# Program order in the first stage of a gated attention and MLP kernel: high halves of splits ahead of low halves, layernorm transposes moved, last stores on three queues

## The chip, the cores and the metric

The kernel runs on one core of a Trainium2 chip. The core has TensorE (PE, matmuls; its weight loads are listed apart as PEld), VectorE (DVE), ScalarE (ACT), GpSimd (POOL) and SyncE (SP, which here only issues DMAs). Each engine takes its instructions in the order of the program. The metric is the device time of one execution in microseconds (us).

## What is computed

With x of 2048 x 448 (all float32), 16 heads of 28, one shared key and value head, and g a sigmoid of x times a gate vector:

```python
q = (x @ wq).reshape(B, S, H, Dh).transpose(0, 2, 1, 3)
k = x @ wk
v = x @ wv
p = softmax(einsum("bhqd,bkd->bhqk", q, k) * Dh ** -0.5)
a = einsum("bhqk,bkd->bhqd", p, v).transpose(0, 2, 1, 3).reshape(B, S, H * Dh) @ wo

h = gelu(layernorm(x) @ w1)
hs = shifted(h) @ w2          # the four quarters of h moved by +1, -1, +2, -2 rows
x1 = x + hs
b = x1 + gelu(layernorm(x1) @ w3) @ w4

out = g * a + (1 - g) * b
```

## The kernel before

The kernel has three stages: q, k, v and the spatial mixer (stage one, to about 140 us), the channel MLP (to about 400 us), and attention with the output projection. The change touches stage one and the last few instructions of stage three.

**Splits.** A float32 product is made of three matmuls of rounded operands: high x high, high x low, low x high. So each operand is split: ACT casts it to its high half (wh, ah, w2h), and DVE subtracts that from the raw value for the low half (wl, al, w2l). `split_w` does it for w1 (high casts, then four subtractions), `split_a` and `split_x` for chunks c0 to c1 of a block of x, `split_w2(m)` for chunk m of w2.

**Blocks.** x is worked in four blocks of 512 rows, b = 0 to 3. `load_x(b)` brings the transposed block (xkv_b), `load_x1(b)` the plain one (x1). The high half of a block stands in a tile `ah` and its low half in `al`, three buffers each, so block 3 takes over those of block 0.

**Steps.** In program order:

- `stage_q(u)`, u = 4b + g: 11 matmuls (`proj`) for 128 columns of q, k and v of block b; `q_out` copies the result on ACT to one of four buffers qf and stores it on ACT's queue to DRAM (qd).
- `ln1_tile(b, t)`: layernorm statistics of tile t of block b on DVE; after t = 3 POOL computes the four scales rs (`stats_end`). The mean is taken out of w1 beforehand (`centre_w1`), so that only rs remains.
- `ln1_send(b)`: PE transposes rs (rsT_b), ACT copies it (rT_b), SP stores it to DRAM. `ln1_read(b)`: SP reads it back as rsb_b, broadcast to 112 partitions.
- `stage_w1(b, between)`: four tiles h_b_m (m = 0 to 3), 11 matmuls each; after each of them `between(m)` is called, then DVE multiplies the result by rsb_b (hf_b_m), ACT takes the Gelu twice (hh, the high half, and hf), and POOL subtracts (hl).
- `stage_w2(b, between)`: four tiles hs_b_t, 12 matmuls each on hh and hl of all four m; DVE adds each to x1, then `between(t)` is called. Tile 3 also reads the first columns of the next block, which POOL copies (L396).
- `stage_kv(b)`: SP reads k and v of block b back from DRAM; `split_k(b)` splits k on POOL.

PE's PSUM tiles for q and h go round four buffers. Everything is in manual schedule: each engine's order is the order of the code, and an instruction waits for what its operands and buffers need.

**The code from q6 to hs_0** calls, before the change: `stage_q(6)`, `centre_w1`, `stage_q(7)`, `split_w` of w1, four `ln1_tile(1, t)`, `stage_q(8)`, `ln1_send(0)`, `stage_q(9)`, `ln1_send(1)`, both `ln1_read`, the loads of block 3, `stage_q(10)`, `stage_q(11)`, `stage_w1(0, split_w2)`, `stage_w1(1, second)`, `stage_kv(0)`, `stage_kv(1)`, `stage_w2(0, third)`. `second(m)` splits block 3 for m = 0 and 1 and takes statistics of block 2 for m = 2 and 3; `third(0)` sends and reads the scales of block 2 and reads k and v of it, `third(1)` to `third(3)` take statistics of block 3.

**The end.** The last four tiles of the output (12 to 15) are computed one after the other; DVE writes 12, 14 and 15, ACT and POOL together 13. Tile 12 is stored from SP's queue, the other three from POOL's. After that every engine loads the flag `redo` (L935) and branches on it (L938) past a repeat of the attention that is not taken in the runs here.

Of the kernel before, what the change touches and what calls it, by code (L numbers as in the profile page):

```python
# [10 lines left out]
F32R = mybir.dt.float32r  # L11
# [5 lines left out]
P = 128  # L17
# [19 lines left out]
def f32(ap):  # L37
    return ap.bitcast(F32)
# [3 lines left out]
def gated_mix_kernel(  # L42
# [12 lines left out]
    nc = tc.nc  # L55
# [20 lines left out]
    first = keep.tile([P, 4], F32, name="first")  # L76
# [28 lines left out]
            nc.vector.tensor_tensor(wl[0:64, 3, cols], raw[0:64, 3, cols], f32(wh)[0:64, 3, cols], ALU.subtract)  # L105
            nc.scalar.copy(wl[64:128, 3, cols], raw[64:128, 3, cols])

    def split_w(raw, wh, wl):
        nc.scalar.copy(wh[:, 0:3, :], raw[:, 0:3, :])
        nc.gpsimd.memset(f32(wh)[64:128, 3, :], 0.0)  # L110
        nc.scalar.copy(wh[0:64, 3, :], raw[0:64, 3, :])
        nc.scalar.copy(wl[64:128, 3, :], raw[64:128, 3, :])
        for c in range(3):
            nc.vector.tensor_tensor(wl[:, c, :], raw[:, c, :], f32(wh)[:, c, :], ALU.subtract)
        nc.vector.tensor_tensor(wl[0:64, 3, :], raw[0:64, 3, :], f32(wh)[0:64, 3, :], ALU.subtract)

    def split_a(raw, ah, al, c0, c1):
        nc.scalar.copy(ah[:, c0:c1, :], raw[:, c0:c1, :])
        c2 = min(c1, 3)
        if c0 < c2:  # L120
            nc.vector.tensor_sub(al[:, c0:c2, :], raw[:, c0:c2, :], f32(ah)[:, c0:c2, :])
        if c1 == 4:
            nc.vector.tensor_sub(ah[64:128, 3, :], raw[64:128, 3, :], f32(ah)[64:128, 3, :])
# [110 lines left out]
    with tc.tile_pool(name="s1b", bufs=1) as s1b, \  # L234
# [13 lines left out]
        xraw, xact = {}, {}  # L248

        def load_x(b):  # L250
            xraw[b] = s1.tile([P, 4, 512], F32, tag="raw", bufs=3, name=f"xkv_{b}")
            nc.sync.dma_start(xraw[b], xT[:, :, 512 * b:512 * b + 512])

        def load_x1(b):
            nc.sync.dma_start(x1[:, 4 * b:4 * b + 4, :],
                              x[512 * b:512 * b + 512, :].rearrange("(t p) d -> p t d", p=P))
# [12 lines left out]
        w2l = s1b.tile([P, 4, D], F32R, name="w2l")  # L269
        hh, hl, acts = {}, {}, {}  # L270

        def split_x(b, c0, c1):
            if b not in xact:
                xact[b] = (s1.tile([P, 4, 512], F32R, tag="ah", bufs=3, name=f"ahk_{b}"),
                           s1.tile([P, 3, 512], F32R, tag="al", bufs=3, name=f"alk_{b}"))
            split_a(xraw[b], *xact[b], c0, c1)

        def q_out(u, ps):
            b, g = divmod(u, NG)
# [16 lines left out]
        def stage_q(u, tile_of=mm1):  # L296
            b, g = divmod(u, NG)
            ps = tile_of(f"q_{u}")
            w = slice(g * P, (g + 1) * P)
            proj(ps, wqh[:, :, w], wql[:, :, w], *xact[b])  # L300
            q_out(u, ps)
# [34 lines left out]
        def ln1_tile(b, t):  # L336
            if t == 0:
                rs1_of[b] = stats_tiles(s1, b)
            stats_tile(s1, b, t, rs1_of[b][0])
            if t == 3:  # L340
                stats_end(*rs1_of[b])

        def ln1_send(b):
            ps = misc_tile(f"rsT_{b}")[0:4, 0:P]
            nc.tensor.transpose(ps, rs1_of.pop(b)[1], ident)
            rT = s1.tile([4, P], F32, tag="rT", bufs=2, name=f"rT_{b}")
            nc.scalar.copy(rT, ps)
            rb_of[b] = dram.tile([4, P], F32, tag="rsd", bufs=2, name=f"rsd_{b}")
            nc.sync.dma_start(rb_of[b], rT)

        def ln1_read(b):
            rd = rb_of[b]
            rb_of[b] = s1.tile([P, 512], F32, tag="rsb", bufs=2, name=f"rsb_{b}")
            nc.sync.dma_start(rb_of[b][0:C], rd.rearrange("(o t) p -> o (t p)", o=1).broadcast_to([C, 512]))
# [14 lines left out]
                nc.vector.scalar_tensor_tensor(w1raw[:, c, :], ps, -1.0 / D, w1raw[:, c, :],  # L369
                                               op0=ALU.mult, op1=ALU.add)  # L370

        def split_w2(m):
            nc.scalar.copy(w2h[0:C, m, :], w2raw[0:C, m, :])
            nc.vector.tensor_tensor(w2l[0:C, m, :], w2raw[0:C, m, :], f32(w2h)[0:C, m, :], ALU.subtract)

        def stage_w1(b, between=None):
            hh[b] = s1b.tile([P, 4, 516], F32R, tag="hh", bufs=2, name=f"hh_{b}")
            hl[b] = s1b.tile([P, 4, 516], F32R, tag="hl", bufs=2, name=f"hl_{b}")
            for m in range(4):
                ps = mm1(f"h_{b}_{m}")  # L380
                w = slice(m * C, (m + 1) * C)
                proj(ps[0:C, :], w1h[:, :, w], w1l[:, :, w], *xact[b])
                if between:
                    between(m)
                hf = s1.tile([P, 512], F32, tag="hf", bufs=3, name=f"hf_{b}_{m}")
                nc.vector.tensor_mul(hf[0:C, :], ps[0:C, :], rb_of[b][0:C, :])
                nc.scalar.activation(hh[b][0:C, m, 2:514], hf[0:C, :], AF.Gelu_apprx_tanh)
                nc.scalar.activation(hf[0:C, :], hf[0:C, :], AF.Gelu_apprx_tanh)
                nc.gpsimd.tensor_tensor(hl[b][0:C, m, 2:514], hf[0:C, :], f32(hh[b])[0:C, m, 2:514],
                                        ALU.subtract)  # L390
            for tt in (hh, hl):
                if b == 0:
                    nc.gpsimd.memset(f32(tt[b])[0:C, :, 0:2], 0.0)
                else:
                    nc.gpsimd.tensor_copy(tt[b][0:C, :, 0:2], f32(tt[b - 1])[0:C, :, 512:514])
                    nc.gpsimd.tensor_copy(tt[b - 1][0:C, :, 514:516], f32(tt[b])[0:C, :, 2:4])  # L396
                if b == NB - 1:
                    nc.gpsimd.memset(f32(tt[b])[0:C, :, 514:516], 0.0)
# [43 lines left out]
        stage_q(6)  # L442
        centre_w1()
        stage_q(7)
        split_w(w1raw, w1h, w1l)
        for t in range(4):
            ln1_tile(1, t)
        stage_q(8)
        ln1_send(0)
        stage_q(9)  # L450
        ln1_send(1)
        ln1_read(0)
        ln1_read(1)
        load_x(3)
        load_x1(3)
        stage_q(10)
        stage_q(11)
        stage_w1(0, split_w2)

        def second(m):  # L460
            if m < 2:
                split_x(3, 2 * m, 2 * m + 2)
            else:
                ln1_tile(2, 2 * m - 4)
                ln1_tile(2, 2 * m - 3)
# [3 lines left out]
        stage_kv(1)  # L469

        def third(t):
            if t == 0:
                ln1_send(2)
                ln1_read(2)
                stage_kv(2)
            else:
                ln1_tile(3, t - 1)

        stage_w2(0, third)
        ln1_tile(3, 3)  # L480
        split_k(0)
        mv0, rs0 = stats_tiles(s1, "m")
# [186 lines left out]
    with tc.tile_pool(name="s3", bufs=1, reuse_waits="tile") as s3, \  # L669
# [220 lines left out]
        def end(t, n, ps, before):  # L890
            if t == 1:
                nc.scalar.activation(y, ps, AF.Copy, scale=gg[:, n:n + 1])
                nc.gpsimd.tensor_tensor(ot_of[n], y, before, ALU.add)
            else:
                nc.vector.scalar_tensor_tensor(ot_of[n], ps, gg[:, n:n + 1], before, op0=ALU.mult, op1=ALU.add)
            queue = nc.sync if t == 0 else nc.gpsimd
            queue.dma_start(out[0, n * P:(n + 1) * P, :], ot_of[n])

        def tail_wo(t):
# [112 lines left out]
```

## Time and profile before

| | us |
|---|---|
| runs of the kernel, median of 3 | 977.44 |
| lowest and highest | 976.42 and 979.18 |
| the profiled execution's own time | 977.92 |
| its span, from the first instruction to the last | 976.1 |
| PE busy | 954.6 (98%) |
| ACT busy | 648.5 (66%) |
| DVE busy | 288.0 (30%) |
| POOL busy | 114.1 (12%) |

Busy times are sums over the span, and stages differ: from 400 to 940 us PE is busy throughout and ACT for 495 of 540 us; from 30 to 60 us PE is busy for 24.84 of 30 us, and from 60 to 80 us for 14.00 of 20. A row of the timeline gives the start, the duration, the engine, the line, the operation and its tiles (out<-in), and in brackets the idle time of the engine before it with what ended it. Matmuls are pipelined: their durations overlap, and the distance of two starts is what one of them costs PE. SPq and ACTq are queues of DMA issues.

### The profile page before, as it was taken

The page shows a single profiled execution, that of the slowest core. Times are in us where ns is not written, and L with a number is a line of the kernel's source. Part 1 is how long each engine was busy: PE and PEld are TensorE (multiplying, and loading weights), DVE is VectorE, ACT ScalarE, POOL GpSimd, SP SyncE. Part 2 cuts the span into 40 slices and gives each one's busy share as a digit, 9 for nine tenths or more (in the row PEclk, how much of TensorE's full clock was granted, in tenths as well). Part 3 has the DMA queues.
Part 4 walks back from the last instruction along what each step waited for, and adds up shares of the span by engine and source line. Part 5 has one row for each costly group of instructions (what it writes and reads, how often), then busy time and mean ns, then how long its engine had stood idle before and what let it go on. Part 6 is the DMA issues. An engine that isn't in the chain of part 4 may idle for free.

```text
span 976.1 us, 13516 instructions
## 1 busy us (share of the span) xinstructions
PE 954.6 (98%) x5191; PEld 636.0 (65%) x5191; DVE 288.0 (30%) x573; ACT 648.5 (66%) x1266; POOL 114.1 (12%) x139
## 2 busy tenths in 40 slices
PE   9779999999999999999999999999999999999996
PEld 6658888888888888855555555555555555545553
DVE  5454354642431431122122222212222221212102
ACT  5352235432232232289999999999999999999994
POOL 3133230200000520040000000000000000000001
PEclk9898999999999999999999999999999999999999
DMA  9810533131120110020110121011021101210101
GB/s 310 260 37 21 137 129 122 41 92 29 26 56 2 38 43 1 10 76 22 40 51 16 36 87 41 22 39 51 22 68 50 42 21 40 69 46 17 40 12 42
DMA packets 44200, 56.24 MB, mean 58 GB/s; under 512 B 9536, under 2 KB 27280, under 8 KB 44128
## 3 DMA queue, kind: packets, MB, share of 16 engines
q1 hardware_dynamic: 41056, 49.37, 17.6%
q10 hardware_dynamic: 2880, 5.24, 1.5%
q8 instruction: 43, 0.70, 0.3%
q0 software_dynamic: 192, 0.69, 0.2%
q14 instruction: 29, 0.24, 0.1%
HBM read 32.19 MB, written 11.67 MB: 45 GB/s over the span
## 4 chain that ended last, share of the span: by engine, by line
PE 93%; ACT 2%; DVE 2%; DMA 1%; issue 1%; POOL 1%; ACTq 0%; POOLq 0%; DVEq 0%
PE bank L831 27%; PE pv L800 24%; PE acc L608 5%; PE acc L610 5%; PE acc L609 5%; PE g L127 4%; PE g L128 4%; PE g L129 4%; PE hs L405 1%; PE hs L406 1%; PE hs L407 1%; PE bank L746 1%; PE bank L744 1%; PE g L130 1%; PE bank L742 1%; PE g L131 1%
## 5 line engine op out<-in xcount | busy, mean ns | idle before, releaser
L833 ACT ACTIVATE p<-bank 128x512 f32<-128x512 f32 x1024 | 511.5, 639 | 34.1 <-PE bank L831 30.9
L831 PE MATMUL bank<-qs,kS 98*128 98x512 f32 x1024 | 306.0, 408 | 0.0
L831 PEld LDWEIGHTS bank<-qs,kS 98*128 98x128 f32 x1024 | 184.3, 189 | 134.1 <-issue 93.1
L800 PE MATMUL pv<-p,vext 128*32 128x512 f32 x2048 | 243.1, 598 | 0.0
L598 ACT ACTIVATE gh<-g 128x512 fp32r<-128x512 f32 x55 | 32.9, 598 | 183.1 <-PE g L131 183.1
L800 PEld LDWEIGHTS pv<-p,vext 128*32 128x32 f32 x2048 | 58.5, 109 | 116.3 <-issue 108.6
L600 DVE TENSOR_TENSOR gl<-gf,gh 128x512 fp32r<-128x512 f32 x55 | 38.3, 696 | 162.5 <-ACT gf L599 158.3
L608 PE MATMUL acc<-w4h,gh 128*128 128x448 f32 x220 | 79.9, 363 | 0.0
L610 PE MATMUL acc<-w4h,gl 128*128 128x448 f32 x220 | 79.9, 363 | 0.0
L609 PE MATMUL acc<-w4l,gh 128*128 128x448 f32 x220 | 79.7, 362 | 0.0
L754 DVE SCALAR_TENSOR_TENSOR ot<-bank,gg,ot 128x448 f32<-128x448 f32 x44 | 30.0, 684 | 143.0 <-ACT p L833 99.3
L127 PE MATMUL g<-ah,w3h 128*128 128x512 f32 x168 | 65.7, 391 | 0.0
L128 PE MATMUL g<-al,w3h 128*128 128x512 f32 x168 | 65.6, 391 | 0.0
L129 PE MATMUL g<-ah,w3l 128*128 128x512 f32 x168 | 65.6, 391 | 0.0
L729 POOL CAST onh<-on 128x512 fp32r<-128x512 f32 x15 | 9.2, 611 | 472.8 <-DVE on L726 472.8
L204 DVE TENSOR_REDUCE mr<-bank 128x4 f32<-128x256 f32 x60 | 25.6, 426 | 105.8 <-PE bank L203 104.7
L609 PEld LDWEIGHTS acc<-w4l,gh 128*128 128x128 f32 x220 | 41.3, 188 | 4.2
L608 PEld LDWEIGHTS acc<-w4h,gh 128*128 128x128 f32 x220 | 41.3, 188 | 4.1
L610 PEld LDWEIGHTS acc<-w4h,gl 128*128 128x128 f32 x220 | 41.3, 188 | 3.0
L708 DVE COPY o<-pv 128x512 f32<-128x512 f32 x15 | 10.4, 692 | 99.4 <-PE pv L800 99.4
L129 PEld LDWEIGHTS g<-ah,w3l 128*128 128x128 f32 x168 | 31.5, 188 | 6.9
L128 PEld LDWEIGHTS g<-al,w3h 128*128 128x128 f32 x168 | 31.5, 188 | 5.6
(193 smaller groups left out, 981.2 us busy)
## 6 DMA issues: line engine op xcount, KB each, us to landing
qs<-qh SPq DMA_DIRECT2D x32, 224.0 KB
qd<-qf ACTq DMA_DIRECT2D x16, 256.0 KB
rb<-rd SPq DMA_DIRECT2D x15, 256.0 KB
x<-in_x_dram SPq DMA_DIRECT2D x4, 896.0 KB
xd<-xt SPq DMA_DIRECT2D x16, 224.0 KB
w34raw<-in_w_dram SPq DMA_DIRECT2D x7, 512.0 KB
qr<-qd SPq DMA_DIRECT2D x16, 224.0 KB
qs<-ql SPq DMA_DIRECT2D x16, 224.0 KB
```

What stands on the lines that cost most here:

```text
L127: nc.tensor.matmul(ps, wh[:, c, :], ah[:, c, :], start=(c == 0), stop=False)
L128: nc.tensor.matmul(ps, wh[:, c, :], al[:, c, :], start=False, stop=False)
L129: nc.tensor.matmul(ps, wl[:, c, :], ah[:, c, :], start=False, stop=False)
L598: nc.scalar.activation(gh, ps, AF.Gelu_apprx_tanh)
L600: nc.vector.tensor_sub(gl, gf, f32(gh))
L608: nc.tensor.matmul(ps, gh[:, tok], w4h[i][:, k, :], start=(f == 0), stop=False)
L609: nc.tensor.matmul(ps, gh[:, tok], w4l[i][:, k, :], start=False, stop=False)
L610: nc.tensor.matmul(ps, gl[:, tok], w4h[i][:, k, :], start=False, stop=(f == stop))
L754: nc.vector.scalar_tensor_tensor(ot_of[n], ps, gg[:, n:n + 1], before, op0=ALU.mult, op1=ALU.add)
L800: nc.tensor.matmul(pv[32 * j:32 * j + 32, :], vext[:, kt, :], ps[j], start=(kt == 0), stop=(kt == NT - 1), tile_position=(0, 32 * j))
L831: nc.tensor.matmul(ps, kS[0:98, kt * P:(kt + 1) * P], q_of[u][0:98, j, :], start=True, stop=True)
L833: nc.scalar.activation(p, ps, AF.Exp, scale=SCALE)
```

## The change

Four things are done.

1. `split_w`, `split_a` and `split_w2` are cut into a high part (ACT) and a low part (DVE), so that they can stand apart in the program. w2's casts for m = 0 and 1 go ahead of `stage_w1(0)`, those for m = 2 and 3 are called after h_0_0 and h_0_1, and block 3's casts (`high_x`) after h_0_2 and h_0_3, where they were in `stage_w1(1)`.
2. `stage_q(8)`, `ln1_send(0)` and `ln1_read(0)` go ahead of w1's split; w1's casts go ahead of the statistics of block 1, w1's subtractions behind them.
3. The transpose of block 1's scales goes from behind q9 to behind h_0_2, with its read; that of block 2's scales from behind hs_0_0 to behind hs_0_2. `stage_kv(2)` goes behind `stage_w2(0)`, and the statistics of block 3 a tile earlier.
4. Of the last four stores, tile 13's stays on POOL's queue, tiles 14 and 15 go to ACT's.

```diff
-    def split_w(raw, wh, wl):
+    def split_w_high(raw, wh, wl):
         nc.scalar.copy(wh[:, 0:3, :], raw[:, 0:3, :])
         nc.gpsimd.memset(f32(wh)[64:128, 3, :], 0.0)
         nc.scalar.copy(wh[0:64, 3, :], raw[0:64, 3, :])
         nc.scalar.copy(wl[64:128, 3, :], raw[64:128, 3, :])
+
+    def split_w_low(raw, wh, wl):
         for c in range(3):
             nc.vector.tensor_tensor(wl[:, c, :], raw[:, c, :], f32(wh)[:, c, :], ALU.subtract)
         nc.vector.tensor_tensor(wl[0:64, 3, :], raw[0:64, 3, :], f32(wh)[0:64, 3, :], ALU.subtract)
...
+        def high_x(b, c0, c1):
+            if b not in xact:
+                xact[b] = (s1.tile([P, 4, 512], F32R, tag="ah", bufs=3, name=f"ahk_{b}"),
+                           s1.tile([P, 3, 512], F32R, tag="al", bufs=3, name=f"alk_{b}"))
+            nc.scalar.copy(xact[b][0][:, c0:c1, :], xraw[b][:, c0:c1, :])
...
-        def split_w2(m):
+        def high_w2(m):
             nc.scalar.copy(w2h[0:C, m, :], w2raw[0:C, m, :])
+
+        def low_w2(m):
             nc.vector.tensor_tensor(w2l[0:C, m, :], w2raw[0:C, m, :], f32(w2h)[0:C, m, :], ALU.subtract)
...
         stage_q(6)
         centre_w1()
         stage_q(7)
-        split_w(w1raw, w1h, w1l)
+        stage_q(8)
+        ln1_send(0)
+        ln1_read(0)
+        split_w_high(w1raw, w1h, w1l)
         for t in range(4):
             ln1_tile(1, t)
-        stage_q(8)
-        ln1_send(0)
+        split_w_low(w1raw, w1h, w1l)
         stage_q(9)
-        ln1_send(1)
-        ln1_read(0)
-        ln1_read(1)
         load_x(3)
+        stage_q(10)
         load_x1(3)
-        stage_q(10)
         stage_q(11)
-        stage_w1(0, split_w2)
+        high_w2(0)
+        high_w2(1)
+
+        def first(m):
+            low_w2(m)
+            if m < 2:
+                high_w2(m + 2)
+            else:
+                high_x(3, 2 * m - 4, 2 * m - 2)
+            if m == 2:
+                ln1_send(1)
+                ln1_read(1)
+
+        stage_w1(0, first)
 
         def second(m):
             if m < 2:
-                split_x(3, 2 * m, 2 * m + 2)
+                split_x(3, 2 * m, 2 * m + 2, False)
...
         def third(t):
-            if t == 0:
+            if t == 2:
                 ln1_send(2)
                 ln1_read(2)
-                stage_kv(2)
-            else:
-                ln1_tile(3, t - 1)
+            if t < 3:
+                ln1_tile(3, t)
 
         stage_w2(0, third)
+        stage_kv(2)
         ln1_tile(3, 3)
...
-            queue = nc.sync if t == 0 else nc.gpsimd
+            queue = (nc.sync, nc.gpsimd, nc.scalar, nc.scalar)[t]
             queue.dma_start(out[0, n * P:(n + 1) * P, :], ot_of[n])
```

PE's order before, at the end of q9 (lines of the kernel before; a number behind a name, as in q_9_366, is a running one):

```order
L130 MATMUL q_9_366<-ahk_2_230,wqh_118 128x512
L131 MATMUL q_9_366<-ahk_2_230,wql_119 128x512
L345 MATMUL rsT_1_381<-ident_67,rs_s1_1_330 4x128
L127 MATMUL q_10_394<-ahk_2_230,wqh_118 128x512
L128 MATMUL q_10_394<-alk_2_231,wqh_118 128x512
```

PE's order now, where that transpose has gone, between the third and the fourth tile of h_0 (lines of the kernel after, where 345 is 358, 127 is 134 and 131 is 138):

```order
L137 MATMUL h_0_2_458<-ahk_0_143,w1h_130 112x512
L138 MATMUL h_0_2_458<-ahk_0_143,w1l_131 112x512
L358 MATMUL rsT_1_474<-ident_67,rs_s1_1_349 4x128
L134 MATMUL h_0_3_487<-ahk_0_143,w1h_130 112x512
L135 MATMUL h_0_3_487<-alk_0_144,w1h_130 112x512
```

The transpose rsT_1 has moved behind q10, q11 and three tiles of h_0; h_0_3 behind it still reads ahk_0, the high half of block 0.

DVE's order before, from the centring of w1 (w1l is w1's low half, st and mv the statistics, here of block 1):

```order
L369 SCALAR_TENSOR_TENSOR w1raw_141<-wsum_ps_300,w1raw_141 128x448 x4
L114 TENSOR_TENSOR w1l_131<-w1raw_141,w1h_130 128x448 x3
L115 TENSOR_TENSOR w1l_131<-w1raw_141,w1h_130 64x448
L135 BN_STATS st_s1_1_0_331<-x1_74 128x6
L136 BN_AGGR mv_s1_1_329<-st_s1_1_0_331 128x2
```

And now:

```order
L382 SCALAR_TENSOR_TENSOR w1raw_141<-wsum_ps_300,w1raw_141 128x448 x4
L142 BN_STATS st_s1_1_0_350<-x1_74 128x6
L143 BN_AGGR mv_s1_1_348<-st_s1_1_0_350 128x2
L142 BN_STATS st_s1_1_1_353<-x1_74 128x6
L143 BN_AGGR mv_s1_1_348<-st_s1_1_1_353 128x2
L142 BN_STATS st_s1_1_2_356<-x1_74 128x6
L143 BN_AGGR mv_s1_1_348<-st_s1_1_2_356 128x2
L142 BN_STATS st_s1_1_3_359<-x1_74 128x6
L143 BN_AGGR mv_s1_1_348<-st_s1_1_3_359 128x2
L116 TENSOR_TENSOR w1l_131<-w1raw_141,w1h_130 128x448 x3
L117 TENSOR_TENSOR w1l_131<-w1raw_141,w1h_130 64x448
```

The four pairs of statistics have gone ahead of the four subtractions, which need ACT's casts.

ACT's order before, from the Gelus of h_0_1, with the waits of each row in brackets (the engine or the DMA semaphore; a row without one needs no wait of its own):

```order
L387 ACTIVATE hh_0_424<-hf_0_1_459 112x512 [waits DVE_49]
L388 ACTIVATE hf_0_1_459<-hf_0_1_459 112x512 [waits Activation_49]
L373 CAST w2h_132<-w2raw_205 112x448
L387 ACTIVATE hh_0_424<-hf_0_2_478 112x512 [waits DVE_49]
L388 ACTIVATE hf_0_2_478<-hf_0_2_478 112x512 [waits Activation_49,Pool_49]
L373 CAST w2h_132<-w2raw_205 112x448
L387 ACTIVATE hh_0_424<-hf_0_3_497 112x512 [waits DVE_49]
```

And now, from the same Gelus:

```order
L402 ACTIVATE hh_0_418<-hf_0_1_453 112x512 [waits DVE_49]
L403 ACTIVATE hf_0_1_453<-hf_0_1_453 112x512 [waits Activation_49]
L289 CAST ahk_3_471<-xkv_3_383 128x1024 [waits DMAHW3_49,PE_49]
L360 COPY rT_1_476<-rsT_1_474 4x128
L402 ACTIVATE hh_0_418<-hf_0_2_482 112x512 [waits DVE_49]
L403 ACTIVATE hf_0_2_482<-hf_0_2_482 112x512 [waits Activation_49,Pool_49]
L289 CAST ahk_3_471<-xkv_3_383 128x1024
L402 ACTIVATE hh_0_418<-hf_0_3_501 112x512 [waits DVE_49]
```

Between the Gelus w2's casts have made room for block 3's casts, the first of which waits for PE, and for the copy of rsT_1, which now stands behind that cast.

More of the change, by code (lines that the diff above doesn't have):

```diff
@@ L115, in split_w, with split_a @@
         nc.vector.tensor_tensor(wl[0:64, 3, :], raw[0:64, 3, :], f32(wh)[0:64, 3, :], ALU.subtract)
-    def split_a(raw, ah, al, c0, c1):
-        nc.scalar.copy(ah[:, c0:c1, :], raw[:, c0:c1, :])
+    def split_w(raw, wh, wl):
+        split_w_high(raw, wh, wl)
+        split_w_low(raw, wh, wl)
+    def split_a(raw, ah, al, c0, c1, high=True):
+        if high:
+            nc.scalar.copy(ah[:, c0:c1, :], raw[:, c0:c1, :])
         c2 = min(c1, 3)
@@ L270, in gated_mix_kernel, with split_x @@
         hh, hl, acts = {}, {}, {}
-        def split_x(b, c0, c1):
+        def split_x(b, c0, c1, high=True):
             if b not in xact:
@@ L275, in split_x @@
                            s1.tile([P, 3, 512], F32R, tag="al", bufs=3, name=f"alk_{b}"))
-            split_a(xraw[b], *xact[b], c0, c1)
+            split_a(xraw[b], *xact[b], c0, c1, high)
+        def high_x(b, c0, c1):
[3 more added lines that the diff above has]
+            nc.scalar.copy(xact[b][0][:, c0:c1, :], xraw[b][:, c0:c1, :])
         def q_out(u, ps):
```

## The prediction

> **What bounds the kernel now.** I read the page's line of granted clock first, then the waits of TensorE (PE), then its timeline from 31 to 84 us. The fence shows the clock in 40 slices; one line of the waits of PE from 20 to 100 us (total, times, longest); two stretches with busy time by engine, granted clock and DMA share; and PE matmuls with start, duration and, in brackets, the idle time before.
>
> ```profile
> PEclk9898999999999999999999999999999999999999
> ...
> PE rsT L345 <- POOL rs_s L140: 11.2, 2, 6.0
> ...
> 37.38:41.95 4.57, 4.56 (x12) 3.60 (x13) 0.00 (x0) 0.26 (x1) 0.00 (x0) 0.50 0.43 95
> 73.57:79.50 5.93, 5.92 (x17) 5.33 (x18) 1.03 (x2) 0.26 (x1) 1.54 (x5) 0.50 0.10 39
> ...
> 31.84 0.39 PE L131 MATMUL q<-ahk,wql 128*128 128x512 f32 x1
> 37.39 0.38 PE L345 MATMUL rsT<-ident,rs_s 128*4 128x128 f32 x1 [5.16 <-POOL rs_s L140]
> 42.13 0.40 PE L127 MATMUL q<-ahk,wqh 128*128 128x512 f32 x1
> 44.65 0.39 PE L127 MATMUL h<-ahk,w1h 128*112 128x512 f32 x1
> 64.96 0.37 PE L405 MATMUL hs<-w2h,hh 112*128 112x448 f32 x1
> 73.58 0.37 PE L345 MATMUL rsT<-ident,rs_s 128*4 128x128 f32 x1 [6.00 <-POOL rs_s L140]
> 79.84 0.37 PE L407 MATMUL hs<-w2h,hl 112*128 112x448 f32 x1
> 83.50 0.37 PE L407 MATMUL hs<-w2h,hl 112*128 112x448 f32 x1
> 83.71 0.40 PE L127 MATMUL h<-ahk,w1h 128*112 128x512 f32 x1
> ```
>
> PE is the bound nearly everywhere. It stops twice, 5.16 and 6.00 us, both times for a tiny transpose, of the layernorm scales of block 1 (rsT_1) and of block 2 (rsT_2). After each stop the granted clock is 0.50 for 4.57 and 5.93 us of full work. So the stops cost 5.16 + 6.00 + half of 4.57 and of 5.93: 16.4 us. In the change rsT_1 stands behind three tiles of h_0, and rsT_2 behind three tiles of hs_0.
>
> **The sum for stage one.** I count again by the starts of matmuls. A q tile takes 44.65 - 42.13 = 2.52. The eight h tiles of blocks 0 and 1 take 64.96 - 44.65 = 20.31, or 2.54 each. The 18 hs matmuls from 79.84 to 83.50 take 0.203 each, so an hs tile of 12 takes 2.44. If PE never waits, q10 starts 0.23 after 31.84, at 32.07; h_0_0 at 37.1, h_0_3 at 44.8, h_1_0 at 47.4, hs_0_0 at 57.5, rsT_2 at 64.9, hs_0_3 at 65.0 and h_2_0 at 67.4. I allow 0.1 for each transpose, which streams 128 columns, a quarter of what takes a q matmul 0.23. Before, h_2_0 started at 83.71: a gain of **16.3 us**, and the other count agrees. The waits of PE from 84 to 400 us have no entry, so what follows moves up with it.
>
> **What has to be ready: the first stop.** ACT, then DVE, from the timeline:
>
> ```profile
> 29.37 1.32 ACT L109 CAST w1h<-w1raw 128x1344 fp32r<-128x1344 f32 x1 [0.45 <-DMA w2raw<-in_w_dram]
> 31.77 0.59 ACT L281 COPY qf<-q 128x512 f32<-128x512 f32 x1
> 32.76 0.26 ACT L347 COPY rT<-rsT 4x128 f32<-4x128 f32 x1 [0.40 <-ACT qf L281]
> 26.91 2.20 DVE L369 SCALAR_TENSOR_TENSOR w1raw<-wsum_ps,w1raw 128x448 f32<-128x448 f32 x4
> 30.73 1.70 DVE L114 TENSOR_TENSOR w1l<-w1raw,w1h 128x448 fp32r<-128x448 f32 x3 [1.62 <-ACT w1h L109]
> 32.87 0.62 DVE L135 BATCH_NORM_STATS2 st_s<-x 128x6 f32<-128x448 f32 x1
> 35.71 0.18 DVE L136 BATCH_NORM_AGGREGATE mv_s<-st_s 128x2 f32<-128x6 f32 x1
> ```
>
> The copy of q8 now stands ahead of the casts of w1. It takes the buffer of q4 and needs that store to be in; at 31.77 it did not wait, so 31.77 is its latest start, and rT_0 keeps 32.76 at the latest. The casts of w1 took 31.77 - 29.37 = 2.4, and now end by 35.4. DVE does the four statistics of block 1 straight after centring w1: 29.1 + 3.0 (32.87 to 35.89) = 32.1. Then w1l, from the end of the first cast at 34.3, takes 1.70 and about a third of that for the half tile: 36.6. PE wants w1h at 37.1 and the first chunk of w1l half a microsecond later. So nothing waits, with 1.7 us to spare. The scales of block 1 took 1.5 us from the statistics to the transpose (35.89 to 37.39) and are there at 33.6, eleven ahead of rsT_1.
>
> **h_0 and h_1.** One line of the waits of DVE from 20 to 90 us, then a round of the old rhythm on DVE, ACT and POOL:
>
> ```profile
> DVE w2l L374 <- ACT w2h L373: 16.1, 4, 10.5
> ...
> 47.37 0.69 DVE L386 TENSOR_TENSOR hf<-h,rsb 112x512 f32<-112x512 f32 x1 [0.31 <-PE h L131]
> 49.88 1.16 DVE L374 TENSOR_TENSOR w2l<-w2raw,w2h 112x448 fp32r<-112x448 f32 x1 [1.82 <-ACT w2h L373]
> 48.10 0.63 ACT L387 ACTIVATE hh<-hf 112x512 fp32r<-112x512 f32 x1 [1.70 <-DVE hf L386]
> 49.30 0.55 ACT L373 CAST w2h<-w2raw 112x448 fp32r<-112x448 f32 x1
> 49.47 1.10 POOL L389 TENSOR_TENSOR hl<-hf,hh 112x512 fp32r<-112x512 f32 x1 [12.14 <-ACT hf L388]
> ```
>
> DVE waited for a cast that stood behind two Gelus on ACT, which stood behind DVE's product: a ring through both engines. With the casts a step ahead, a tile takes DVE 1.16 + 0.69 = 1.85, ACT 2 x 0.63 + 0.55 = 1.8 and POOL 1.10, all under PE's 2.54, so all three keep up.
>
> **The added wait.** The cast of block 3, high_x(3, 0, 2), takes the oldest of three ah buffers, which h_0_3 still reads. The order shows the wait on PE, and none on rT_1 behind it, which needs one too: so it is for a matmul later than rsT_1. ACT stands until h_0_3 ends, 47.6. Behind it are queued rT_1 and the Gelus of h_0_2 and h_0_3; for rT_1 wait the broadcast rsb_1, DVE's products of h_1, the statistics of block 2 behind these, and rsT_2. Durations, on ACT, DVE, SP's queue, GB/s in 40 slices of 74 to 80 us (the transfer of rsb), and POOL:
>
> ```profile
> 60.18 1.03 ACT L118 CAST ahk<-xkv 128x1024 fp32r<-128x1024 f32 x1
> 65.48 0.75 DVE L121 TENSOR_TENSOR alk<-xkv,ahk 128x512 fp32r<-128x512 f32 x1 [2.36 <-ACT ahk L118]
> 66.25 0.69 DVE L123 TENSOR_TENSOR ahk<-xkv,ahk 64x512 fp32r<-64x512 f32 x1
> 74.27 0.25 SPq L349 DMA_DIRECT2D rsd<-rT  x1
> 75.46 0.30 SPq L354 DMA_DIRECT2D rsb<-rsd  x1
> GB/s 0 0 0 0 0 0 10 3 0 0 0 0 0 0 0 0 0 55 164 205 191 178 164 191 164 137 41 41 0 0 0 0 0 0 0 0 0 0 0 0
> 74.92 0.19 POOL L396 CAST hl<-hl 112x8 fp32r<-112x8 f32 x1
> ```
>
> 47.6 + 1.03 + 0.26 is 48.9 for rT_1; 1.2 later (74.27 to 75.46) rsb_1 is issued, 50.1; its bytes flow until 2.7 after the issue, I take 3.1 to the semaphore: 53.2. The product of h_1_0 starts there, 3.1 later than its matmuls allow. Then DVE: product 0.7, split 0.75 + 0.69, product 0.7, two statistics 1.5, product 0.7, two statistics 1.5, product 0.7: the third product ends at 58.2, the statistics at 59.7, the last product at 60.4. On POOL hl_1_2 ends 1.3 + 1.1 after 58.2, at 60.6, and the scales by 62.1: rsT_2 at 64.9 has 2.8 to spare. hl_1_3 and four casts of 0.19 end by 64.0: hs_0_3, which reads the last of them, has **1.0** to spare at 65.0. So I cost the wait at nothing. If that cover goes, PE waits at hs_0_3 for the difference.
>
> The loads xkv_3 and x1 of block 3 stand behind rsb_0 on SP and go earlier than before; the k and v rows stand behind rsb_1 and go later, but POOL wants them only after h_2 has begun.
>
> **The last stores.** DVE's last products, then the store line's forms (durations; first and last start) and its times to landing, then branch and load instructions at the end:
>
> ```profile
> 968.08 1.29 DVE L895 SCALAR_TENSOR_TENSOR ot<-bank,gg,ot 128x448 f32<-128x448 f32 x2
> L897 POOL DMA_DIRECT2D out_dram<-ot x3: 542/545/767, 969.5 to 970.8; - x3
> DMA to landing us min/median/max: 3.9/3.9/4.1
> L935 ACTq TENSOR_LOAD <-redo x1: 723/723/723, 968.0 to 968.0; - x1
> L938 PEldq COMPARE_BRANCH  x1: 4202/4202/4202, 968.9 to 968.9; - x1
> ```
>
> The last store lands at 970.8 + 3.9 = 974.7, and the span ends at 976.1. Now only out tile 13 is POOL's, issued at 969.5 and in by 973.6; ACT issues the others from 968.8 and 969.4. PE's branch ends at 973.1 as before. ACT loads redo 1.7 later; should its branch cost what PE's does, it ends by 974.8. So the edit gains between nothing and 1.6; I take **1.0**, nearest to the landing row. The Trainium skill (DMA: Bandwidth & Descriptors, Issuing engines are not separate DMA queues) speaks against more: queues of several engines share the same DMA engines, and spreading saves only time to issue. By that the gain would be an estimated 1.3, the way from 969.5 to 970.8; no run here shows it yet.
>
> **Total.** 16.3 + 1.0 = 17.3. The profiled execution took 977.9 (span 976.1), so 960.6; the median of the runs lies 0.5 below it, so 960.1. I say **960.4**.
>
> **Rivals.** *Cover lost at hs_0_3.* If rsb_1 comes 2 to 5 us later than 53.2, because loads of block 3 still fill the queues, PE waits 1 to 4 us there: 961.4 to 964.4. For it: only 1.0 of slack, and a DMA in the way of every number. Against it: those loads start ten microseconds ahead. After such a short stop the half clock could add up to half of 5.93; no row shows one. The Trainium skill (TensorE: Matmul & The Clock Gate, Part 1: The HAM clock gate) wants an idle window of some 3.4 us before the clock halves; the stops of 5.16 and 6.00 agree, and by that a short one would cost itself alone. 20%.
>
> *The first stop comes back for w1.* If the casts end over 1.7 us late, h_0_0 waits by what is over; with the old stop's 5.16 and its half clock, 7.4 at most: 961 to 968. 5%.
>
> *No gain.* The stops would be work, not order: DVE, ACT and POOL full in that stretch, and PE waiting elsewhere for as long. Each round above says no. 977; 2%.
>
> *Slower.* One mechanism: rsb_1 stuck behind other transfers. From 1.0 of slack on, each microsecond costs one, and 3.0 come on top for the half clock; the gain of 17.3 is used up when it lands some 15 later than taken, 18 after its issue, six times the 3.1 of that row. At 20 after its issue the time would be 979.5. 1%.
>
> **How the numbers follow.** Forecast 72%, 959 to 961.5; the rivals 28%. For 8 in 10 I take the lost cover in, and below it the upper end of the stores and the spread of runs: 958.0 to 964.5. Faster than before by over 0.3% (about what a measurement of this kernel can tell from no change), below 974.5: 0.96; within it 0.02; slower 0.02.
>
> **What would show it.** Right: PE's waits have no line for rsT, the clock line shows no half clock after the start, h_2_0 starts near 67.4, and the last store is issued before 970. Wrong: a wait of PE at hs_0_3 for POOL's cast, an idle before h_0_0, or a span that ends more than 1.5 us after the last landing.

## The result, and the profile after

The changed kernel takes 961.84 us (median of four runs, 960.32 to 962.56), the kernel before beside it on the same chip 978.31. The ratio is 0.9831, with a 95% interval of 0.9810 to 0.9853. The prediction was 960.4, with a range of 958.0 to 964.5. The profiled execution took 962.56, with a span of 960.7 (before: 977.92 and 976.1).

The page's line of granted clock of the changed kernel, in 40 slices:

```profile
PEclk9999999999999999999999999999999999999998
```

The slices at 8 near the start (the second and the fourth) are gone, and one has come at the very end. Of the waits of PE between 20 and 100 us nothing is left: rsT had 11.2 us there. PE's timeline of the changed kernel, rows at the places that the prediction names:

```profile
37.29 0.39 PE L134 MATMUL h<-ahk,w1h 128*112 128x512 f32 x1
44.91 0.27 PE L358 MATMUL rsT<-ident,rs_s 128*4 128x128 f32 x1
57.76 0.37 PE L420 MATMUL hs<-w2h,hh 112*128 112x448 f32 x1
65.10 0.27 PE L358 MATMUL rsT<-ident,rs_s 128*4 128x128 f32 x1
67.67 0.39 PE L134 MATMUL h<-ahk,w1h 128*112 128x512 f32 x1
```

None has a bracket, so none waited. h_0_0 was forecast at 37.1, hs_0_0 at 57.5, rsT_2 at 64.9 and h_2_0 at 67.4: each came 0.2 to 0.3 late. From 83.71 to 67.67, stage one gained 16.04 us. The next row is the start of the tail, the first copy of o on ACT, before and then after:

```profile
963.05 0.78 ACT L904 COPY o<-pv 128x128 f32<-128x128 f32 x4 [1.76 <-PE pv L800]
```

```profile
946.96 0.78 ACT L931 COPY o<-pv 128x128 f32<-128x128 f32 x4 [1.76 <-PE pv L827]
```

963.05 - 83.71 is 879.34 and 946.96 - 67.67 is 879.29: all between the two stretches stayed as it was. But the tail, from this copy to the end of the span, took 13.05 before and takes 13.74 now. Here a microsecond should have been gained, and 0.69 were lost. The view by windows (length, PE busy with its matmuls, granted clock, DMA share, GB/s), of before and of after, each cut where the clock could change:

```profile
960.16:963.57 3.41, 2.95 (x23) 1.00 0.00 0
963.57:966.98 3.41, 2.72 (x14) 1.00 0.00 0
966.98:970.39 3.41, 1.66 (x9) 1.00 0.24 79
970.40:973.81 3.41, 0.00 (x0) 1.00 0.61 214
```

```profile
946.44:949.85 3.41, 2.25 (x13) 1.00 0.00 0
949.85:953.26 3.41, 3.41 (x11) 0.50 0.16 59
953.26:956.67 3.41, 0.85 (x4) 1.00 0.42 144
```

After, the clock is halved for 3.41 us while PE does the last matmuls of wo. DVE's last products start 953.54 - 946.96 = 6.58 behind the first copy of o, before 968.08 - 963.05 = 5.03:

```profile
953.54 1.30 DVE L922 SCALAR_TENSOR_TENSOR ot<-bank,gg,ot 128x448 f32<-128x448 f32 x2 [0.58 <-PE bank L773]
```

So the tail holds 1.55 us of half clock, and without it would be 0.9 shorter than before. The question for the experiments was whether those 0.9 are the stores, whether the half clock belongs to the change, and what the parts of stage one bring each.

### The profile page after: what moved, and what is told of

Its sections match the earlier page's. It is cut to its first block, busy times and chain, and to the rows that moved or that the text cites. A ratio compares the mean times of both kernels' runs of the same rounds, so it can differ in the third digit from the quotient of the medians.

```text
span 960.7 us, 13515 instructions
## 1 busy us (share of the span) xinstructions
PE 951.1 (99%) x5191; PEld 633.4 (66%) x5191; DVE 286.6 (30%) x573; ACT 648.2 (67%) x1266; POOL 113.1 (12%) x137
## 4 chain that ended last, share of the span: by engine, by line
PE 98%; DMA 0%; POOL 0%; ACT 0%; DVE 0%; issue 0%; ACTq 0%
PE bank L858 27%; PE pv L827 24%; PE acc L635 5%; PE acc L637 5%; PE acc L636 5%; PE g L134 4%; PE g L135 4%; PE g L136 4%; PE hs L421 1%; PE bank L773 1%; PE bank L771 1%; PE hs L420 1%; PE hs L422 1%; PE bank L769 1%; PE g L137 1%; PE g L138 1%
```

## The experiments

What they are read by, from each kernel's one profiled execution, with the same differences of starts as above (h_0_0 from the first matmul of wsum_ps, 23.64 before and 23.62 after; the tail from the first copy of o to the end of the span). The median of e11 is a single run:

| kernel | first eight q matmuls | h_0_0 from wsum | h_0_0 to h_2_0 | tail | half clock in the tail | median |
|---|---|---|---|---|---|---|
| before | 3.70 | 21.01 | 39.06 | 13.05 | no | 978.31 |
| changed | 3.70 | 13.67 | 30.38 | 13.74 | yes | 961.84 |
| e1, first transpose alone | 3.70 | 13.42 | 39.71 | 13.26 | no | 971.22 |
| e2, second alone | 6.22 | 20.64 | 34.38 | 12.44 | no | 974.27 |
| e3, casts in step | 6.35 | 13.42 | 34.38 | 13.20 | yes | 965.71 |
| e4, sent a tile later | 3.70 | 13.41 | 30.61 | 13.85 | yes | 962.28 |
| e5, stores alone | 4.56 | 20.08 | 38.75 | 11.82 | no | 977.35 |
| e6, stores as before | 3.70 | 13.41 | 30.38 | 12.78 | no | 962.11 |
| e7, stores from SP | 3.70 | 13.41 | 30.38 | 12.60 | no | 963.11 |
| e8, tail filled | 3.70 | 13.42 | 30.37 | 13.07 | no | 961.06 |
| e9, changed again | 3.70 | 13.43 | 30.38 | 13.51 | yes | 961.41 |
| e10, tail and start filled | 3.70 | 13.42 | 30.38 | 12.24 | no | 960.74 |
| e11, sent earlier | 3.70 | 14.75 | 30.38 | 13.05 | no | 962.67 |
| e12, sent two tiles later | 4.38 | 13.42 | 31.78 | 12.91 | no | 963.29 |

### Parts of stage one: e1, e2, e3

**e1**, on the kernel before:

```diff
         stage_q(9)
-        ln1_send(1)
         ln1_read(0)
-        ln1_read(1)
...
-        stage_w1(0, split_w2)
+        def first(m):
+            split_w2(m)
+            if m == 2:
+                ln1_send(1)
+                ln1_read(1)
+
+        stage_w1(0, first)
```

> The kernel before with one edit: the sending of block 1's scales (rsT_1, rT_1, rsd_1, rsb_1) stands behind the third tile of h_0. Theory (each stop costs itself and half of the half-clock stretch behind it): the stop of 5.16 and half of 4.57 us go, h_2_0 starts 7.4 us earlier than the 83.71 of before, at 76.3, and the second stop stays at about 6 us with its half clock; the time falls by 7.4 us. Rival (the stops are work of DVE and ACT in the old ring, not order): PE meets the ring sooner, the second stop grows by what the first gave, and the time falls by under 3 us.

971.22 beside 977.18 for the kernel before, ratio 0.9926 (0.9904 to 0.9949). h_0_0 comes 7.59 earlier, but the second stop became dearer. PE's timeline of e1, and the windows behind that stop:

```profile
66.50 0.37 PE L345 MATMUL rsT<-ident,rs_s 128*4 128x128 f32 x1 [6.51 <-POOL rs_s L140]
76.62 0.40 PE L127 MATMUL h<-ahk,w1h 128*112 128x512 f32 x1
```

```profile
66.50:72.80 6.30, 6.30 (x19) 0.53 0.10 37
```

The stop is 6.51 instead of 6.00. A mean clock of 0.53 over 6.30 us is a half clock over some 5.9, as long as before. From wsum, h_2_0 gains 60.07 - 53.13 = 6.94. The theory (7.4) holds but for half a microsecond; the rival's 3 is out, for the runs give 7.2 (5.0 to 9.4).

**e2**, on the kernel before:

```diff
-            if t == 0:
+            if t == 2:
                 ln1_send(2)
                 ln1_read(2)
-                stage_kv(2)
-            else:
-                ln1_tile(3, t - 1)
+            if t < 3:
+                ln1_tile(3, t)
 
         stage_w2(0, third)
+        stage_kv(2)
```

> The kernel before with one edit: rsT_2 stands behind the third tile of hs_0, and the k and v rows of block 2 behind hs_0. Theory: the scales are there at 73.5 and POOL's last cast of hl_1 ends at 75.1 whatever PE does, so of the stop of 6.0 us some 2.8 stay, in two waits, too short to be followed by a half clock: h_2_0 starts at 77.6, 6.1 us earlier than before, and the first stop stays. Rival (moving the transpose is the whole gain): all of 9.0 us go, h_2_0 at 74.7. Rival (the half clock follows a stop of 2.8 us too): about 4 to 5 us.

974.27, ratio 0.9959 (0.9939 to 0.9980). From h_0_0 to h_2_0 it takes 34.38, 4.68 less than before. PE's timeline and windows of e2:

```profile
74.44 0.47 PE L405 MATMUL hs<-w2h,hh 112*128 112x448 f32 x1 [2.36 <-DVE x L409]
78.44 0.38 PE L345 MATMUL rsT<-ident,rs_s 128*4 128x128 f32 x1
```

```profile
74.40:75.40 1.00, 0.96 (x4) 0.92 0.00 0
75.40:78.80 3.40, 3.40 (x11) 0.52 0.00 0
78.80:81.10 2.30, 2.30 (x13) 1.00 0.00 1
```

Two things came otherwise than the theory said. PE stops at hs_0_2, for DVE's addition of hs_0_0 to x1: the tiles of hs have two buffers, and that addition is queued on DVE behind the last product of h_1. And a half clock does follow a stop of 2.36 us, about a microsecond behind its end. The third case of the expectation, 4 to 5 us, is what the profile shows; the runs give 4.0 (2.0 to 6.0).

**e3**, on the changed kernel:

```diff
-        high_w2(0)
-        high_w2(1)
...
         def first(m):
+            high_w2(m)
             low_w2(m)
-            if m < 2:
-                high_w2(m + 2)
-            else:
-                high_x(3, 2 * m - 4, 2 * m - 2)
...
-                split_x(3, 2 * m, 2 * m + 2, False)
+                split_x(3, 2 * m, 2 * m + 2)
```

> The changed kernel with one part undone: ACT's casts of w2 and of block 3 stand in the same step as DVE's subtractions again, all transposes where the change puts them. Theory (the order of the casts carries what the two moves do not): DVE's products of h_0 come every 3.6 us instead of 2.54, the scales of block 2 are ready at 66.2 and POOL's last cast of hl_1 ends at 67.7, where the changed kernel has 62.3 and 63.9; PE waits 2.6 us in all before hs_0_3, h_2_0 starts at 70.3 instead of 67.7, and the time is 2.6 us longer than the changed kernel's. Rival (the moves of the transposes are all, four buffers of h take up the ring): h_2_0 at 67.7 and the changed kernel's time. Rival (a short stop brings the half clock too): 4 to 6 us longer.

965.71, ratio 0.9868 (0.9843 to 0.9893); the changed kernel had 0.9831 and, in e9, 0.9843. The intervals overlap, so the runs alone do not tell e3 from the changed kernel, and what follows is read from one profile each. There h_0_0 to h_2_0 takes 34.38, 4.0 more than in the changed kernel. DVE's, PE's timeline and windows of e3:

```profile
65.97 0.67 DVE L401 TENSOR_TENSOR hf<-h,rsb 112x512 f32<-112x512 f32 x1
66.56 0.61 DVE L424 TENSOR_TENSOR x<-x,hs 128x448 f32<-128x448 f32 x1
```

```profile
67.22 0.47 PE L420 MATMUL hs<-w2h,hh 112*128 112x448 f32 x1 [2.20 <-DVE x L424]
73.88 0.40 PE L134 MATMUL h<-ahk,w1h 128*112 128x512 f32 x1
```

```profile
68.70:71.10 2.40, 2.40 (x9) 0.50 0.00 0
```

The place is again hs_0_2: the addition ends at 67.17, PE starts at 67.22. The stop of 2.20 and the half clock behind it make the 4.0. So the casts put a step ahead carry 4.0 us of the 16.3 in such a run, and the two moves without them the rest; the last case of the expectation, 4 to 6 us, came at its lower end. The half clock need not follow in every run: the mean granted clock of e3's four runs goes from 0.995, the slowest and the one shown here, to 0.998. e1's and e2's gains also show it: 6.94 + 4.68 is 11.6, not 16.3.

### The added wait: e4, e12, e11

**e4** and **e12** send block 1's scales one and two tiles later, **e11** puts the sending ahead of the cast that waits:

```diff
# e4
-            if m == 2:
+            if m == 3:
                 ln1_send(1)
                 ln1_read(1)
# e12
         def second(m):
+            if m == 0:
+                ln1_send(1)
+                ln1_read(1)
# e11
             low_w2(m)
+            if m == 2:
+                ln1_send(1)
+                ln1_read(1)
             if m < 2:
                 high_w2(m + 2)
             else:
                 high_x(3, 2 * m - 4, 2 * m - 2)
-            if m == 2:
-                ln1_send(1)
-                ln1_read(1)
```

> The changed kernel with the sending of block 1's scales one tile later, behind the fourth tile of h_0 instead of the third. It measures the cover of the added wait, taken as 1.0 us in the prediction and read as 1.3 us in the changed kernel's trace (POOL's last cast ends at 63.85, hs_0_3 starts at 65.12). Theory: rT_1 goes 2.5 us later, behind ACT's second cast of block 3, rsb_1 lands at 56.0 instead of 53.6, DVE's last product of h_1 ends at 62.9 instead of 60.5, rsT_2 still does not wait (0.3 us left), and hs_0_3 waits 1.2 us for POOL's cast; h_2_0 starts 1.2 us later, the time is 1.2 us longer and no half clock follows. Rival (more cover than thought, because DVE catches up while PE is bound): no change. Rival (a half clock follows a short stop): 2 to 4 us longer.

> The changed kernel with the sending of block 1's scales two tiles later, behind h_1_0. In e4, one tile later, DVE's first product of h_1 came 1.3 us later, hs_0_2 waited 0.2 us for DVE's add of hs_0_0 (two buffers of hs), and h_2_0 stood 0.2 us later than in the runs without a wait. Theory (from there on each microsecond costs one): rT_1 stands behind the Gelus of h_0_3 and comes 1.35 us later than in e4, hs_0_2 waits 1.5 to 1.7 us, and h_2_0 stands 45.4 behind the first matmul of wsum if no half clock follows so short a stop; 47.1 if it does, as it did behind the 2.20 us of e3. Rival (slack is left elsewhere): 44.0 to 44.5.

> The changed kernel with rT_1 on ACT ahead of the cast of block 3 that waits for h_0_3, so that the wait the change adds delays no scales. Theory (the wait costs nothing, as predicted): rT_1 goes at 45.2 instead of 48.7, the first product of h_1 at 50.4 instead of 53.7, DVE's add of hs_0_0 no longer stands behind a late product, and h_2_0 stays 43.8 us behind the first matmul of wsum. Rival (the wait does cost something): h_2_0 up to 0.3 us earlier than in the changed kernel.

DVE's timeline of the changed kernel, the first and last product of h_1 and the addition behind it:

```profile
53.68 0.69 DVE L401 TENSOR_TENSOR hf<-h,rsb 112x512 f32<-112x512 f32 x1 [3.60 <-POOL hl L408]
...
59.85 0.67 DVE L401 TENSOR_TENSOR hf<-h,rsb 112x512 f32<-112x512 f32 x1
60.44 0.61 DVE L424 TENSOR_TENSOR x<-x,hs 128x448 f32<-128x448 f32 x1
```

The addition ends at 61.05. The bracket names a memset of POOL, but in e4 the same memset stands at 53.08 and the first product at 54.96: what that product waits for is taken to be the scales. PE's timeline of e4, where the last product came 1.67 us later against h_0_0, and of e12, 2.85 later:

```profile
62.04 0.37 PE L422 MATMUL hs<-w2h,hl 112*128 112x448 f32 x1
62.39 0.47 PE L420 MATMUL hs<-w2h,hh 112*128 112x448 f32 x1
```

```profile
64.13 0.47 PE L420 MATMUL hs<-w2h,hh 112*128 112x448 f32 x1 [1.17 <-DVE x L424]
66.68 0.27 PE L358 MATMUL rsT<-ident,rs_s 128*4 128x128 f32 x1
69.25 0.39 PE L134 MATMUL h<-ahk,w1h 128*112 128x512 f32 x1
```

e4 lost 0.23 (30.61 against 30.38), where its theory had 1.2 at hs_0_3: the first to be late is hs_0_2 by 0.15, the gap between 62.24 and 62.39. e12 lost 1.40, close to its theory, and its clock stayed at 1.00:

```profile
64.00:66.00 2.00, 1.87 (x9) 1.00 0.00 0
66.00:68.00 2.00, 2.00 (x12) 1.00 0.00 0
```

So the cover of the wait is about 1.45 us (1.67 of delay cost 0.23, 2.85 cost 1.40), it ends at hs_0_2, and from there a microsecond costs one. In e11 rT_1 went at 46.16 and the first product waited for its matmuls and no longer for the scales, and h_0_0 to h_2_0 stayed 30.38: with the order of the change, the wait costs nothing. e11's own time is long for another reason, earlier in the program. Its PE waits at rsT_0, whose PSUM buffer is the one that wsum_ps was in:

```profile
30.61 0.27 PE L358 MATMUL rsT<-ident,rs_s 128*4 128x128 f32 x1 [1.18 <-DVE w1raw L382]
```

There the split of block 2 started on DVE at 22.13, in the kernel before at 20.78, and everything behind it was as much later. In the changed kernel's own profile it started at 21.19, and cost the 0.25 by which its 13.67 stands above the 13.42 of the others.

### The stores and the tail: e5, e6, e7, e8, e9, e10

**e5** puts only the last stores on three queues, **e6** takes only that back, **e7** uses SP instead of ACT:

```diff
# e5, on the kernel before
-            queue = nc.sync if t == 0 else nc.gpsimd
+            queue = (nc.sync, nc.gpsimd, nc.scalar, nc.scalar)[t]
# e6, on the changed kernel
-            queue = (nc.sync, nc.gpsimd, nc.scalar, nc.scalar)[t]
+            queue = nc.sync if t == 0 else nc.gpsimd
# e7, on the changed kernel
-            queue = (nc.sync, nc.gpsimd, nc.scalar, nc.scalar)[t]
+            queue = nc.gpsimd if t == 1 else nc.sync
```

> The kernel before with the last stores alone changed: out tile 12 from SP, 13 from POOL, 14 and 15 from ACT. As predicted: 1.0 us less from the first copy of o to the span's end (13.05 us before), with the last landing by 973.6. Theory from the changed kernel's trace: the stores gain 0.9 us where the clock stays whole in the tail, and what ends last is ACT, which issues two DMAs, loads redo 1.7 us later than before and ends its branch 3 us after that; where the clock is halved in the tail, that costs 1.5 us more whatever the stores are. Rival: the stores gain nothing or lose, because ACT's branch takes the place of the landings.

> The changed kernel with the last stores as before: tile 12 from SP, the other three from POOL. Theory: 0.9 us longer than the changed kernel where the tail's clock is the same, with POOL's third landing last again. Rival (the stores lost 0.6 us): 0.6 us shorter. The half clock over the last matmuls of wo comes or stays away without regard to the stores.

> The changed kernel with out tiles 14 and 15 from SP's queue instead of ACT's. Theory (ACT's late load of redo and its branch end the program): ACT ends with its y as before, SP issues both in some 0.35 us each, the last landing is then what ends last, about 3.8 us behind DVE's last product, and the span ends 0.6 to 1.1 us earlier than in the changed kernel where the tail's clock is the same. Rival (whichever engine issues last pays the same for load and branch): no change within 0.3 us.

**e8** and **e10** fill PE in the tail, e10 also at the start; **e9** is the changed kernel again, beside e10:

```diff
# e8 and e10
+        def keep_clock(n):
+            for _ in range(n):
+                nc.tensor.matmul(tq[3], warm[:, 0:P], warm[:, 0:P], start=True, stop=True)
+        keep_clock(6)
         for t in range(4):
             nc.tensor.transpose(tp[t // 2][:, t % 2], o[:, toks[t]], ident)
+        keep_clock(4)
...
         tail_back(1)
+        keep_clock(4)
...
+        keep_clock(2)
         tail_back(3)
# e10 too
-    for _ in range(16):
+    for _ in range(18):
         nc.tensor.matmul(wps[:, 0:256], warm[:, 0:P], warm, start=True, stop=True)
```

> The changed kernel with 16 matmuls added in the tail, 128 columns each of a tile of zeros, into a bank that the fourth transpose overwrites later: 6 ahead of the transposes of o, 4 behind them, 4 and 2 between the transposes of the normalised rows. They compute nothing of the result. Theory (the half clock from 949.85 to 953.26 follows the thin stretch of PE between the last pv matmul and the first wo matmul, and costs 1.5 us when it comes): with PE busy there no run shows the half clock in the tail; the last product of DVE stands 5.0 us behind the first copy of o in every trace instead of 6.6, less 0 to 0.4 us that the added matmuls delay PE; the median is 0.3 to 1.2 us lower. Rival (the half clock has nothing to do with how full PE is): it stays as often, and the time is 0 to 0.4 us longer.

> The changed kernel once more, beside the next one on one chip. Its runs differ by which half clock falls on it: none in the tail or 1.55 us of it, and 3.7 or up to 6.3 us for the first eight matmuls of q. So a median between 960.5 and 962.5, a spread of 2 to 4 us, and h_2_0 43.8 to 44.1 us behind the first matmul of wsum in the profile.

> The changed kernel with the 16 matmuls in the tail, as in e8, and 18 instead of 16 matmuls of zeros ahead of the first q, so that PE is busy until its first data land at 5.0 to 5.4 us. Neither computes anything of the result. Theory (both spreads are the half clock, and follow a thin stretch of PE): the tail's clock stays whole in every run and the first eight matmuls of q take 3.7 us in most; median 960 to 961, some 1 us below the changed kernel's. Rival (the start is slow for another reason, such as the order in which loads arrive): as many runs with a slow start as before, and the median equals that of e8, 961.1.

**The stores.** e5 against the kernel before is 1.0001 (0.9991 to 1.0012; twelve runs against sixteen): the edit alone is worth 0 with about 1.0 to either side. e6 is 0.9844 (0.9829 to 0.9859), e7 0.9851 (0.9833 to 0.9869), and the changed kernel in e9 0.9843 (0.9825 to 0.9861): no difference either. In the tails with a whole clock, the four profiles with the old stores take 12.44 to 13.26, mean 12.9, the five with the new ones 11.82 to 13.07, mean 12.6, e7 12.60. So 0.3 us by the means, in a spread of 1.25. What became of the rest shows in the store line's times to landing, which it gives for POOL's stores alone, in the changed kernel and then in e8, where POOL issued at 953.2:

```profile
DMA to landing us min/median/max: 3.6/3.6/3.6
```

```profile
DMA to landing us min/median/max: 5.2/5.2/5.2
```

The same transfer took 3.6 to 5.2 us. In e8, 953.2 + 5.2 is 958.4, and the span ends 1.4 later, at 959.8. In all ten profiles with a whole clock in the tail the span ends 1.4 to 1.5 behind POOL's last landing. POOL's last issue did come earlier by what the move promised: 6.5 behind the first copy of o instead of 7.7 to 7.8. But the landing took longer: 3.3 to 4.0 for the last of the old stores (before, e1, e2, e6; mean 3.7), and 3.9 to 5.2 for POOL's with the new ones and a whole clock (e5, e7, e8, e10, e11, e12; mean 4.7). So 1.0 of the 1.3 was lost again on the way to DRAM. That the stores, issued closer together, hold each other up fits this, and no run shows it. In the changed kernel's profile POOL's store had landed by 958.1, but ACT was late. Its stores, its branch, and the semaphore behind it:

```profile
L924 ACTq DMA_DIRECT2D out_dram<-ot x2: 348/833/1318, 954.3 to 954.9; - x2
...
L965 ACTq COMPARE_BRANCH  x1: 54/54/54, 956.8 to 956.8; - x1
...
L965 ACTq EVENT_SEMAPHORE  x1: 17/17/17, 959.8 to 959.8; - x1
```

ACT's branch stands 9.8 behind the first copy of o (before 968.8 - 963.05 = 5.8), and its semaphore comes 3.0 after the branch. The second issue took 1.32 us; with the clock whole (e5, e8, e10, e11, e12) it took 0.35, in the other profiles with a half clock 0.55, 0.99 and 1.04. Why it is slower there no run tells. e7, which takes ACT out, did not make the time shorter: its landing took 4.7.

**The half clock in the tail.** It lay on four of the twelve profiles whose tail is not filled (changed, e3, e4, e9). All four have the new stores, but so have e11 and e12, which do not have it; and the stretch that decides is over (949.85) before the first of these stores is issued (951.88, on SP). In e6 and e7, with no stop in stage one either, the runs have mean granted clocks of 0.995 to 0.999, like those of e9. So it is taken not to be the stores. What does tell the four from the eight is how busy PE was in one step of 3.41 us over the thin stretch, the steps being those in which each trace's clock changes. In changed, e3, e4 and e9 the least busy step that reaches into it has 2.25 to 2.30 us of PE; in the other eight it has 2.42 to 2.72. The nearest two, e9 (halved behind it) and e1 (not):

```profile
946.10:949.51 3.41, 2.30 (x11) 1.00 0.00 0
```

```profile
956.46:959.87 3.41, 2.42 (x11) 1.00 0.00 0
```

The four kernels whose first stage is wholly or partly the old one (before, e1, e2, e5) had no half clock there, but with one profile each that may be chance. In e8 the thin stretch is filled. Its windows:

```profile
946.70:949.70 3.00, 2.73 (x25) 1.00 0.00 0
949.70:953.10 3.40, 2.62 (x14) 1.00 0.18 67
```

DVE's last products start 5.02 behind the copy of o, and the mean granted clock is 0.999 in all five runs of e8, where the five of e9 have 0.996 to 0.999. That is what its theory asked for. In the median it is not shown: e8 has 0.9829 (0.9814 to 0.9844), the changed kernel 0.9831 beside other runs. e10, with the start filled as well, has 960.74 (960.47 to 961.78) against e9's 961.41 (961.03 to 964.52) on the same chip; the ratios to before, 0.9834 (0.9820 to 0.9847) and 0.9843 (0.9825 to 0.9861), overlap. e10 is the fastest median here, and not shown to be faster than the changed kernel.

**The start.** The first eight matmuls of q take 3.70 us in ten of fourteen profiles and 4.38, 4.56, 6.22 and 6.35 in the others, whatever the kernel. The later wsum_ps of those runs is as much later, so this alone moves a run by up to 2.65 us. The views show a clock of 1.00 there, but they count time without an entry in the trace's list of clock periods as whole. That list begins at 4.02 to 5.16 us in the ten, ahead of their first q matmul, and in e12, e5, e2 and e3 at 6.46, 6.80, 10.38 and 10.50, behind it. If the clock was half until then, the eight matmuls take 3.70 and half of the time from the first of them to that entry: 4.40, 4.59, 6.25 and 6.39. That is what was measured, to 0.04, so the slow start is a half clock too. Whether e10's two more matmuls prevent it is not shown, since most profiles without them start as fast.

## Why the prediction was right, and where it was not

- **Two stops and their half clocks, 16.3 us: right.** Measured 16.04 in the profile of the changed kernel; against the 13.42 + 30.38 from wsum of e6, e9 and e10 it is 60.07 - 43.80 = 16.27. The missing quarter is a load that came 0.4 us late. That the size fits so closely is partly luck: the length of a half clock differs from run to run. In e5, whose first stage is that of the kernel before, it lay over 3.4 us of work behind the first stop instead of 4.57, and h_2_0 came 58.83 behind wsum instead of 60.07.
- **The first stop: right.** h_0_0 did not wait for w1, and rsT_0, rT_0 and the casts came in the order worked out. The prediction missed that rsT_0 has little room behind DVE's reading of wsum_ps; e11 shows that a late load comes through there.
- **h_0 and h_1 at PE's pace: right.** DVE's products of h_0 came 2.53 to 3.15 us apart, and e3 shows the old ring back when the casts go back: a stop at hs_0_2.
- **The added wait, costed at nothing: right in size, wrong in its cover.** rT_1 was forecast at 48.9 and came at 48.73, the last product of h_1 at 60.4 and ended at 60.52, the casts at 64.0 and ended at 63.85. But "hs_0_3 ... has 1.0 to spare" named the wrong place. The step left out DVE's addition of hs_0_0, queued behind that last product, which hs_0_2 needs two tiles on: e4 and e12 stop there, with a cover of about 1.45.
- **The last stores, 1.0 us: mis-sized.** The step took a landing of 3.9 as fixed. The edit by itself is worth 0 with an interval of about 1.0 to either side (e5), 0.3 by the tails: POOL's last issue came 1.3 earlier and its landing took 1.0 longer. Where the clock was halved, ACT took the landing's place: "should its branch cost what PE's does" was the right doubt, left at too little. The prediction's own sign of an error, a span ending over 1.5 us after the last landing, is there: 960.7 against 958.1. The Trainium skill (DMA: Bandwidth & Descriptors, Issuing engines are not separate DMA queues) said that spreading over engines saves only time to issue; e5 agrees, with less than the estimate of 1.3 made from it (its interval ends at a gain of 0.9).
- **What no step had: half a clock in the tail**, 1.55 us in four of twelve profiles. Both kernels have the thin stretch, so it is no part of the gain; it fell on the profiled execution after and not on that before. The 1.55, less the 0.9 by which the tail is shorter otherwise, makes the tail's 0.69 the wrong way.
- **Rivals.** The lost cover did not come, nor a wait for w1. The half clock behind a short stop, allowed as half of 5.93 but doubted, is real: in e2 and e3 it follows stops of 2.36 and 2.20. That a short stop "would cost itself alone" did not hold there; it did in e12, whose stop was 1.17.

The gain beside the kernel before, 978.31 - 961.84 = 16.47, is 0.8 short of the 17.3 of the sum, which the stores' missing 0.7 to 1.0 would explain; but its interval, 14.4 to 18.6, is too wide to show that. The rest of the 1.4 us between 960.4 and 961.84 is within what the kernel before itself varied, 977.44 when the forecast was made and 978.31 here.

## What to carry to other kernels

A stop of the bound engine is priced with the half clock that can follow it, and moving the instruction that stops is only half the work: the engines that feed it must be put a step ahead too, or a smaller stop comes back one wait further on (e2, e3). When a wait is added, follow what is queued behind it to every buffer that the bound engine will want, not only to the operand that is computed last. A microsecond at the very end of a program is worth a measurement before it is worth an edit: here the stores left 1.3 us earlier and landed 1.0 later, and the clock varies by more.

## What the runs showed of the hardware

The clock changes in steps of 3.41 us here: after, at 949.85, 953.26 and 956.67, and the half clocks of stage one last one to three such steps (6.83 us before, from 35.15 to 41.97; 10.24 in e1; 3.41 in e2). It falls behind a step in which PE stood still for a part, and the step need not be idle throughout. The step ahead of e2's half clock, and the one that holds the stop of e12, which no half clock followed:

```profile
71.82:75.23 3.41, 1.05 (x6) 1.00 0.00 0
```

```profile
61.07:64.48 3.41, 2.24 (x12) 1.00 0.09 29
```

So a stop of 1.17 us (e12) was followed by no half clock, stops of 2.20 and 2.36, which fell almost wholly into one step, were. The busy time of PE alone does not give the limit. In the tail, over the same thin stretch, steps with 2.25 to 2.30 us were followed by a half clock and steps with 2.42 to 2.72 were not; but a step with 1.66 us of the wo matmuls was not followed by one either (before, 966.98 to 970.39, where the clock stays whole until 973.81). What is counted beside it no run shows. The same thin stretch is hit or missed by where such a step happens to lie.

The Trainium skill (TensorE: Matmul & The Clock Gate, Part 1: The HAM clock gate) gives a window of 3413 ns that runs freely, and the traces agree with 3.41. It lets the clock fall after an idle window of about that length; these runs show falls after windows in which PE was busy for 1.05 (e2) and 2.25 us (after), so here the measurement decides.

ACT's branch at the end of the program is followed by 2.4 us (e7) to 3.2 us (e9) until its semaphore, though the branch itself is 50 to 54 ns; PE's branch is shown as 3.4 to 4.7 us long. Work given to an engine just ahead of it moves that end with it: ACT's semaphore stands 8.3 us behind the first copy of o before, and 10.3 in e5, which gives ACT two stores and has a whole clock there too.
